# Seven block products instead of eight in the output product of a maxout layer, with the sums on VectorE

## The chip, the cores and the metric

The kernel runs on one core of a Trainium2 chip. The metric is the device time of one execution in microseconds (us). PE is TensorE, DVE is VectorE, ACT is ScalarE, POOL is GpSimd, SP is SyncE, whose queue issues most of the transfers.

## What is computed

Two layers, one after the other. The first is a DeltaNet attention, a recurrence over 768 positions with a state of 48 x 48 per head, for 4 sequences and 8 heads. The second is a maxout layer on the 3072 tokens that come out, with 384 features each:

```python
for t in range(S):
    y[:, :, t] = np.einsum('bhd,bhde->bhe', q[:, :, t], state)
    v_old = np.einsum('bhde,bhd->bhe', state, kt)
    state = state + bt[:, :, :, None] * np.einsum('bhd,bhe->bhde', kt, vt - v_old)
...
h = np.maximum(np.maximum(x @ w1, x @ w2), x @ w3)
return (h @ w_out).astype(np.float32)
```

x is 3072 x 384, w1 to w3 are 384 x 768, w_out is 768 x 384. All is FP32.

## The kernel before, in words

The positions are taken in chunks of 64, which turns the recurrence into matrix products and one triangular system of 64 x 64 per chunk and head. Six groups of two chunks follow one another. A group has 512 tokens (4 sequences, two chunks of 64 positions), so that the maxout layer of a group has four sets of 128 tokens.

The order of all instructions is written by hand: the program order is the order on every engine and on every queue. `ffn(m)` (L903) makes the maxout layer of group m and yields between its products. At each yield the loop over `ffn(m)` (L1173 to L1186) puts in pieces of other work: the recurrence of group m+1 by the table `LINKS` (L1064), and steps of the triangular solve of group m+2 by `some(solving, n)` (L1186).

`ffn(m)` for a group from the second on:
- Yields 0 to 11: for each of six sets of 128 hidden features, the products with w2 - w1 and w3 - w1 (L914, `p_h`, 3 products of 512 columns each). ScalarE takes the first with a Relu (L924), VectorE the second with a maximum (L928). The hidden values are six tiles `h` of 128 x 512. The part h takes from w1 is added afterwards: `both_layers` (L891, called in the second group) multiplies w1 by w_out once, and the result lies in `w_sb[0][:, :, 0:384]`.
- Yields 12 to 19: the output product (L938 to L956). For each of four sets of 128 tokens, `p_o` sums six products of h with w_out and three of x (`xt`) with w1 w_out, each of 384 columns (L946). ScalarE copies `p_o` to `o_sb` (L952), and SyncE stores it (L955). There is a yield within each set and one after it.

`p_h`, `p_o` and `p_m` share two PSUM buffers with the tag "ffn" (L81), which are used in turn. The work of the recurrence uses three others ("two").

VectorE's part of the solve, `solve(m)` (L498): norms, then 31 steps of a product (L552, to `tmp`, two buffers) and a subtraction (L556), of 31 to 256 columns, each of which needs the one before it. Then SyncE stores the result (L577) and reads it back transposed into `ut` (L586), for which `join_z` (L694, letter z) of the next group waits at its yield 3. The solve of group m+2 begins at yield 8 of `ffn(m)`, with one step there and three at each later yield. Groups 4 and 5 (counted from 0) have no solve beside them.

Other work at the yields that the text names: y1 (`to_y`, L793, VectorE adds `p_y` at L803), x1 (`y_blocks`, L833, stores y), w0 and w1 (`read_y`, reads it back), X0 and X1 (`turn_y`, L857, VectorE's transposes into the next group's `xt`, L861), s1 (`step`, L771, VectorE adds `p_s` to the state, L789), u1 (`new`, `p_u`, L759), k1 and q1 (L738, L747; VectorE subtracts `p_k` from `v_t`, L743), P0 (`prep_values`, GpSimd scales `v_t`, L287), K0 to K3 (loads of keys on GpSimd's queue, L120). "square" (L308) is a ring of 17 tiles of 128 x 512 for h and the recurrence's intermediates.

Of the kernel before, what the change touches and what calls it, by code (L numbers as in the profile page):

```python
# [9 lines left out]
FP32 = mybir.dt.float32  # L10
# [4 lines left out]
ALU = mybir.AluOpType  # L15

C = 64
# [6 lines left out]
def kernel(  # L24
# [47 lines left out]
    work = ctx.enter_context(tc.tile_pool(name="work", bufs=2))  # L72
# [7 lines left out]
    def ps_ffn(shape, name):  # L80
        return psum.tile(shape, FP32, name=name, tag="ffn", bufs=2)  # L81
# [27 lines left out]
    def rows(bb):  # L109
        return slice(C * bb, C * (bb + 1))  # L110
# [77 lines left out]
    t1 = [const.tile([128, 2, H, BL], FP32, name=f"t1{i}") for i in range(NU)]  # L188
# [118 lines left out]
    def square(name):  # L307
        return work.tile([128, H, C], FP32, name=name, tag="square", bufs=17)  # L308
# [189 lines left out]
    def solve(m):  # L498


        x = in_rows(xs[m])
# [38 lines left out]
        for j in range(size - 1):  # L540
            a, b = j + 1, size - 1 - j
            n = BL // size
            tmp = work.tile([128, 256], FP32, name="tmp")
            t_v = tmp[:, 0 : n * a * b].rearrange("p (s c i) -> p s c i", s=n, i=b)
            row, column, rest = (
                xv[:, :, j, None, j + 1 : size],
                yv[:, :, 0:a, j, None],
                yv[:, :, 0:a, j + 1 : size],
            )
            if n == 1:  # L550
                row, column, rest, t_v = (t[:, 0] for t in (row, column, rest, t_v))
            nc.vector.tensor_tensor(  # L552
                out=t_v, in0=row.to_broadcast(t_v.shape),
                in1=column.to_broadcast(t_v.shape), op=ALU.mult,
            )
            nc.vector.tensor_tensor(out=rest, in0=rest, in1=t_v, op=ALU.subtract)  # L556
            if m == 1 and j == BL - 8:
                nc.scalar.copy(done[:, :, 0:HB], y[:, :, 0:HB])
            elif m == 1 and j == BL - 2:
                nc.vector.tensor_copy(done[:, :, HB:BL], y[:, :, HB:BL])  # L560
            yield
        if m == 0:
# [3 lines left out]
            for i in range(4):  # L566
                if i % 2:
                    n = H * (i == 3)
# [7 lines left out]
        for cc in range(2):  # L576
            nc.sync.dma_start(  # L577
                out=y_d[cc].rearrange("f b h i j -> (f b h) i j"),
                in_=done[64 * cc : 64 * (cc + 1)],
            )  # L580
        yield
        for cc in range(2):
            for half in range(2):
                for bb in range(2):
                    r0 = C * bb + BL * half
                    (one_queue if m or cc else both_queues)[bb].dma_start(  # L586
                        out=ut[cc][
                            r0 : r0 + BL, :, :, BL * half : BL * (half + 1)
                        ].rearrange("p g h i -> p (g h) i"),
                        in_=y_d[cc, half, 2 * bb : 2 * bb + 2].rearrange(  # L590
                            "b h c i -> c (b h) i"
                        ),
# [126 lines left out]
    xts, rhss, qss, us, yts = {}, {}, {}, {}, {}  # L719
# [171 lines left out]
    def both_layers(t):  # L891
        p_m = ps_ffn([128, DM], "p_m")
        for f in range(FT):
            nc.tensor.matmul(  # L894
                p_m,
                w_sb[0][:, t, f * 128 : (f + 1) * 128],
                wo_sb[:, f],
                start=(f == 0),
                stop=(f == FT - 1),
            )  # L900
        nc.scalar.copy(w_sb[0][:, t, 0:DM], p_m)

    def ffn(m):  # L903
        xt = xts[m]
        hs = {}

        def hidden(f, lo, w):
            if f not in hs:
                hs[f] = square("h").rearrange("p h c -> p (h c)")
            h = hs[f][:, lo : lo + w]  # L910
            for i in range(m > 0, 3):
                p_h = ps_ffn([128, TOK], "p_h")[:, 0:w]
                for t in range(KT):
                    nc.tensor.matmul(  # L914
                        p_h,
                        w_sb[i][:, t, f * 128 : (f + 1) * 128],
                        xt[:, t, lo : lo + w],
                        start=(t == 0),
                        stop=(t == KT - 1),
                    )  # L920
                if i == 0:
                    nc.scalar.copy(h, p_h)
                elif m and i == 1:
                    nc.scalar.activation(  # L924
                        out=h, in_=p_h, func=mybir.ActivationFunctionType.Relu
                    )
                else:
                    nc.vector.tensor_tensor(out=h, in0=h, in1=p_h, op=ALU.max)  # L928
                yield


        early = FT // 2 if m == 0 else 0
        for lo in (0, TOK // 2):
            for f in range(early):
                yield from hidden(f, lo, TOK // 2)
        for f in range(early, FT):
            yield from hidden(f, 0, TOK)
        for i in range(4):  # L938
            cc, g = divmod(i, 2)
            p_o = ps_ffn([128, DM], "p_o")  # L940
            last = slice(i * 128, (i + 1) * 128)
            terms = [(hs[f][:, last], wo_sb[:, f]) for f in range(FT)]
            if m:
                terms += [(xt[:, t, last], w_sb[0][:, t, 0:DM]) for t in range(KT)]
            for n, (stays, moves) in enumerate(terms):
                nc.tensor.matmul(  # L946
                    p_o, stays, moves, start=(n == 0), stop=(n == len(terms) - 1)
                )
                if m and n == 4:
                    yield  # L950
            o_sb = work.tile([128, DM], FP32, name="o_sb")
            nc.scalar.copy(o_sb, p_o)  # L952
            for bb in range(2):
                tok0 = (2 * bb + g) * S + (2 * m + cc) * C
                nc.sync.dma_start(out=out[tok0 : tok0 + C, :], in_=o_sb[rows(bb)])  # L955
            yield  # L956
# [3 lines left out]
    def some(gen, n):  # L960
        for _ in range(n):
            if next(gen, gen) is gen:
                break

    conv = weights()
    solving = solve(0)
    zeros(*(t[:, :, :, D:DP] for t in kmore), qall[:, :, :, D:DP])
    for t in (*ut, st):
# [69 lines left out]
    for _ in range(2):  # L1038
# [15 lines left out]
    to_y(0)  # L1054
    halves_t(1)
    solving = solve(1)
    some(solving, 1)
    to_x(0)
# [5 lines left out]
    LINKS = {  # L1064
# [3 lines left out]
    }  # L1068
    EARLY_LINKS = {
# [19 lines left out]
        t=turn, K=load_k, L=lambda n: load_blocks(n, nc.sync),  # L1089
        g=lambda n: gram(n, queues=(nc.gpsimd,) * 2 if n in (10, 11) else one_queue),  # L1090
# [29 lines left out]
    for i, _ in enumerate(ffn(0)):  # L1120
# [17 lines left out]
        if i == 20:  # L1138
            solving = solve(2)
            some(solving, 1)  # L1140
# [32 lines left out]
    for m in range(1, GROUPS):  # L1173
        for i, _ in enumerate(ffn(m)):
            if i == 0:
                some(solving, 3)
            if m == 1 and i in (2, 5, 8):
                both_layers(i // 3)
            if m + 2 < GROUPS:
                if i == 6:  # L1180
                    blocks(m + 2)
                if i == 8:
                    solving = solve(m + 2)
            links(m + 1, LINKS.get(i, ""))
            if i > 7:
                some(solving, 3 if i > 8 else 1)  # L1186
    by_hand.close()
# [1 line left out]
_INS = ['q', 'k', 'v', 'beta', 'moe_w1', 'moe_w2', 'moe_w3', 'moe_w_out']  # L1189
# [26 lines left out]
```

## Time and profile before

| | |
|---|---|
| median of 3 runs | 518.06 us (516.55 to 520.37) |
| the profiled execution, its own time | 523.32 us |
| its span, first to last instruction | 521.3 us |
| TensorE busy | 496.0 us (95%) |
| VectorE, GpSimd, ScalarE busy | 306.0, 192.6, 163.3 us |
| L914 `p_h`, instructions, busy | 522, 220.7 us |
| L946 `p_o`, instructions, busy | 288 with h (97.7 us), 120 with x (42.0 us) |
| L552 and L556, the solve's steps | 139 and 139 instructions on `y_bl`, 51.4 and 48.5 us |
| L952, ScalarE's copies of `p_o` | 24, 11.5 us, 479 ns each |
| mean granted clock of TensorE | 0.966 |

Every matrix product of FP32 operands stands in the profile as two instructions: 204 products `p_o` in the program are 408 rows. "Busy" is the time in which an engine has an instruction in flight. In a timeline row the numbers are the start, the time from the start of the first to the end of the last instruction in it, the engine and the line; in brackets stands the idle time before it and what ended it. Durations of TensorE's rows run into one another, so that the distance from start to start is the time that a product takes.

### The profile page before, as it was taken

What the parts mean: (1) busy time and instruction counts of PE and PEld (TensorE: products, weight loads), DVE (VectorE), ACT (ScalarE), POOL (GpSimd) and SP (SyncE); (2) the same over time, 40 slices, a digit from 0 to 9 for tenths busy, and PEclk for the clock granted to TensorE, in tenths of its full rate; (3) what the DMA queues carried; (4) which work ended last, traced back from release to release, by engine and by line L of the source; (5) the groups of instructions that cost most, each with busy time, mean ns of one, the idle gap of its engine ahead of it and who ended that gap; (6) DMA issues with size and microseconds to landing.
All of it is one profiled execution on the core that took longest, in us unless ns stands there. A gap on an engine that the chain in (4) does not pass through costs nothing.

```text
span 521.3 us, 18005 instructions
## 1 busy us (share of the span) xinstructions
PE 496.0 (95%) x7836; PEld 306.0 (59%) x7836; DVE 306.0 (59%) x689; ACT 163.3 (31%) x302; POOL 192.6 (37%) x317
## 2 busy tenths in 40 slices
PE   7578799998999999999999999999999999999996
PEld 6467688755565555665555565555655555654453
DVE  5888969867996430998642987635896321111100
ACT  4575755883422242201243101252101411011000
POOL 6435462783391926670665680503130000000000
PEclk9956989999999999999989999999999999999999
DMA  8927969764055925353675354823343202220011
GB/s 116 205 37 208 209 136 149 189 192 106 2 132 141 180 49 130 102 129 84 148 126 123 107 144 95 169 38 92 83 106 83 41 3 63 62 60 0 0 30 30
DMA packets 105277, 53.45 MB, mean 103 GB/s; under 512 B 89712, under 2 KB 98960, under 8 KB 105200
## 3 DMA queue, kind: packets, MB, share of 16 engines
q1 hardware_dynamic: 93616, 31.55, 30.0%
q0 software_dynamic: 9472, 20.37, 15.9%
q8 instruction: 61, 1.00, 0.8%
q10 hardware_dynamic: 2112, 0.39, 0.5%
q14 instruction: 16, 0.13, 0.1%
HBM read 39.17 MB, written 13.11 MB: 100 GB/s over the span
## 4 chain that ended last, share of the span: by engine, by line
PE 80%; DMA 7%; DVE 6%; ACT 2%; issue 2%; SPq 2%; POOL 1%; DVEq 0%; ACTq 0%; POOLq 0%
PE p_h L914 35%; PE p_o L946 26%; PE p_g L406 2%; PE p_u L759 2%; PE p_m L894 2%; PE p_k L731 2%; PE p_q L731 2%; PE p_y L801 2%; DMA kmore<-in_k_dram 2%; PE p_s L782 2%; PE p_j L714 2%; DMA x_bl<-at_d 2%; DMA qall<-in_q_dram 1%; DMA ut<-y_d 1%; SPq L120 1%
## 5 line engine op out<-in xcount | busy, mean ns | idle before, releaser
L914 PE MATMUL p_h<-xt,w_sb 128*128 128x512 f32 (+1 forms) x522 | 220.7, 567 | 1.9 <-issue 1.2
L914 PEld LDWEIGHTS p_h<-xt,w_sb 128*128 128x128 f32 x522 | 96.6, 194 | 88.2 <-issue 81.1
L946 PE MATMUL p_o<-wo_sb,h 128*128 128x384 f32 x288 | 97.7, 489 | 0.0
L928 DVE TENSOR_TENSOR h<-h,p_h 128x512 f32<-128x512 f32 (+1 forms) x48 | 29.6, 617 | 93.6 <-PE p_h L914 93.0
L946 PEld LDWEIGHTS p_o<-wo_sb,h 128*128 128x128 f32 x288 | 53.7, 190 | 35.7 <-issue 0.5
L552 DVE TENSOR_TENSOR tmp<-x_bl,y_bl 128x31 f32<-128x31 f32 (+20 forms) x139 | 51.4, 370 | 4.1
L952 ACT COPY o_sb<-p_o 128x384 f32<-128x384 f32 x24 | 11.5, 479 | 132.1 <-PE p_o L946 126.0
L556 DVE TENSOR_TENSOR y_bl<-y_bl,tmp 128x31 f32<-128x31 f32 (+20 forms) x139 | 48.5, 349 | 4.8
L924 ACT ACTIVATE h<-p_h 128x512 f32<-128x512 f32 x30 | 17.9, 597 | 90.3 <-PE p_h L914 87.3
L946 PE MATMUL p_o<-w_sb,xt 128*128 128x384 f32 x120 | 42.0, 486 | 0.0
L364 POOL DMA_DIRECT2D turned<-in_q_dram x72 | 39.3, 554 | 5.4 <-POOL turned L359 3.1
L254 POOL TENSOR_TENSOR w_sb<-mant,up 128x384 int32<-128x384 int32 x18 | 18.8, 1046 | 41.1 <-DVE mant L250 39.0
L946 PEld LDWEIGHTS p_o<-w_sb,xt 128*128 128x128 f32 x120 | 22.8, 190 | 15.9
L406 PEld LDWEIGHTS p_g<-kqt 48*64 48x64 f32 x1216 | 24.3, 141 | 9.9 <-issue 6.4
L406 PE MATMUL p_g<-kqt 48*64 48x64 f32 (+1 forms) x1216 | 27.5, 240 | 0.9 <-ACT kqt L335 0.8
L120 POOL DMA_DIRECT2D kpad<-in_k_dram x32 | 21.9, 692 | 13.8 <-issue 12.7
L789 DVE TENSOR_TENSOR st<-st,p_s 48x768 f32<-48x768 f32 (+1 forms) x18 | 17.1, 950 | 15.3 <-PE p_s L782 15.1
L139 POOL DMA_DIRECT2D v_t<-in_v_dram x14 | 11.6, 832 | 38.1 <-PE p_u L759 38.1
L390 DVE TENSOR_TENSOR pt<-p_g,mask 128x512 f32<-128x512 f32 x20 | 13.8, 689 | 16.1 <-PE p_g L406 15.8
L287 POOL TENSOR_TENSOR v_t<-v_t,nrm 128x768 f32<-128x768 f32 x12 | 17.9, 1495 | 9.0 <-DVE nrm L281 8.9
L359 POOL MEMSET turned<- 128x96 f32 x18 | 3.3, 192 | 46.6 <-DVE kqt L380 46.6
L759 PEld LDWEIGHTS p_u<-v_t,ut 64*64 64x64 f32 x768 | 14.2, 149 | 8.9 <-issue 6.4
(143 smaller groups left out, 616.4 us busy)
## 6 DMA issues: line engine op xcount, KB each, us to landing
out_dram<-o_sb SPq DMA_DIRECT2D x48, 96.0 KB, 2.2
w_bits<-in_moe_w_dram SPq DMA_DIRECT2D x9, 384.0 KB, 6.0
w_bits<-in_moe_w_dram POOLq DMA_DIRECT2D x9, 384.0 KB, 5.6
turned<-in_q_dram POOLq DMA_DIRECT2D x72, 48.0 KB, 2.8
kpad<-in_k_dram POOLq DMA_DIRECT2D x32, 96.0 KB, 5.9
y_x<-y SPq DMA_DIRECT2D x16, 192.0 KB
qall<-y_x SPq DMA_DIRECT2D x32, 96.0 KB, 2.6
v_t<-in_v_dram POOLq DMA_DIRECT2D x14, 192.0 KB, 4.8
```

The lines of the kernel that those rows point to most:

```text
L120: queues[bb].dma_start(out=dst[rows(bb ^ g), :, 0:D], in_=src[2 * bb + g, :, c * C : (c + 1) * C, :].rearrange("h p d -> p h d"),)
L254: nc.gpsimd.tensor_tensor(out=dst.bitcast(I32), in0=mant_v.bitcast(I32), in1=up_v, op=ALU.add)
L287: nc.gpsimd.tensor_tensor(out=vts[c], in0=vts[c], in1=nrm[:, :, :, None].to_broadcast([128, 2, H, D]), op=ALU.mult,)
L364: (queue, nc.gpsimd)[i].dma_start(out=t[p0 : p0 + 32, bb, at : at + NP * 2 * D].rearrange("p (j x) -> p j x", j=NP), in_=(k, q)[i][2 * bb ...
L406: nc.tensor.matmul(p_g[rows(bb ^ (g * i)), par, c0 : c0 + C * (1 + whole)], kq[:, 0], kq if whole else kq[:, i],)
L552: nc.vector.tensor_tensor(out=t_v, in0=row.to_broadcast(t_v.shape), in1=column.to_broadcast(t_v.shape), op=ALU.mult,)
L556: nc.vector.tensor_tensor(out=rest, in0=rest, in1=t_v, op=ALU.subtract)
L731: nc.tensor.matmul(p_b[rows(bb), par, c0 : c0 + D], kqt[g][dims(par), j, bb ^ g, i], st[dims(par), bb ^ g, g, j],)
L759: nc.tensor.matmul(p_v[rows(bb ^ g), g, i], ut[c % NU][rows(bb), g, h], rhs[rows(bb), g, h],)
L914: nc.tensor.matmul(p_h, w_sb[i][:, t, f * 128 : (f + 1) * 128], xt[:, t, lo : lo + w], start=(t == 0), stop=(t == KT - 1),)
L928: nc.vector.tensor_tensor(out=h, in0=h, in1=p_h, op=ALU.max)
L946: nc.tensor.matmul(p_o, stays, moves, start=(n == 0), stop=(n == len(terms) - 1))
```

## The change

From the second group on, `ffn` leaves the output product to a new function, `outputs`. It takes h as 2 x 2 blocks (256 tokens of one chunk by 384 hidden features: a11, a12, a21, a22, each three tiles of 128 x 256) and w_out as 2 x 2 blocks (384 hidden features by 192 columns), and makes the product of the two by Winograd's form of Strassen's scheme: seven block products instead of eight. Each block product is six products of 192 columns: two sets of 128 tokens, three tiles of hidden features. The four products of x with w1 w_out, also of 192 columns, are summed in PSUM with a12 b21, with s124 b22 and with a22 t4; the fourth stands alone.

The sums of blocks of h and of the results are made by VectorE: twelve of 128 x 256 (six s, then three and three that change s in place) and eight of 128 x 384 per group. Four PSUM tiles per group are copied by ScalarE, and four are taken by VectorE within a sum. The sums of blocks of w_out are made once, by `cross_weights` at yields 9 and 10 of the second group, partly into the columns of `w_sb[0]` that are no longer used. Each of the four output blocks (256 tokens by 192 columns) is stored by two transfers on SyncE's queue.

`outputs` has eleven yields instead of eight, so that the table `LINKS` and the number of solve steps per yield are changed: three steps up to yield 12, then two, and three at the last. `tmp` has one buffer instead of two.

```diff
-            tmp = work.tile([128, 256], FP32, name="tmp")
+            tmp = work.tile([128, 256], FP32, name="tmp", bufs=1)
...
+    def cross_weights(part):
+        left, right = slice(0, HALF), slice(HALF, DM)
+        top, bottom = wo_sb[:, 0:PAIRS], wo_sb[:, PAIRS:FT]
+        spare = w_sb[0][:, :, DM : 2 * DM]
+        minus = nc.vector.tensor_tensor
+        if part == 0:
+            minus(
+                out=spare[:, :, right], in0=bottom[:, :, right], in1=top[:, :, right],
+                op=ALU.subtract,
+            )
+            minus(
+                out=top[:, :, right], in0=top[:, :, right], in1=top[:, :, left],
+                op=ALU.subtract,
+            )
+            return
+        minus(
+            out=spare[:, :, left], in0=bottom[:, :, right], in1=top[:, :, right],
+            op=ALU.subtract,
+        )
...
+        for j in range(PAIRS):
+            minus(
+                out=fourth[j], in0=wo_sb[:, PAIRS + j, left], in1=spare[:, j, left],
+                op=ALU.subtract,
+            )
...
+    def outputs(m, hs):
+        xt, w = xts[m], crossed
+        a11, a21, a12, a22 = (
+            [hs[j + d][:, lo : lo + 256] for j in range(PAIRS)]
+            for d, lo in ((0, 0), (0, 256), (PAIRS, 0), (PAIRS, 256))
+        )
+        p, q = (ps_ffn([128, 2, HALF], "p_o") for _ in range(2))
+        def times(to, a, b, start=True, stop=True):
+            for g in range(2):
+                for j in range(PAIRS):
+                    nc.tensor.matmul(
+                        to[:, g], a[j][:, 128 * g : 128 * (g + 1)], b[j],
+                        start=(start and g == j == 0),
+                        stop=(stop and g == 1 and j == PAIRS - 1),
+                    )
...
+        times(p, a11, w["b11"])
+        m1 = held("m1", 1)
+        nc.scalar.copy(m1, p)
+        yield
+        sums = [square("s").rearrange("p h c -> p (h c)") for _ in range(PAIRS)]
+        s124, s3 = ([s[:, lo : lo + 256] for s in sums] for lo in (0, 256))
+        for j in range(PAIRS):
+            op(s3[j], a11[j], a21[j], minus)
+        for j in range(PAIRS):
+            op(s124[j], a21[j], a22[j], plus)
+        times(q, a12, w["b21"], True, False)
+        yield
+        x_times(q, 0, 0)
+        c11 = held("o_sb", 2)
+        op(c11, m1, q, plus)
+        store(c11, 0, 0)
+        yield
+        times(p, s3, w["t3"])
+        m7 = held("o_sb", 2)
+        nc.scalar.copy(m7, p)
+        yield
+        times(q, s124, w["t1"])
+        m5 = held("up", 2)
+        nc.scalar.copy(m5, q)
+        for j in range(PAIRS):
+            op(s124[j], s124[j], a11[j], minus)
+        yield
+        x_times(p, 0, 1, True, False)
+        yield
+        times(q, s124, w["t2"])
+        m6 = held("up", 2)
+        nc.scalar.copy(m6, q)
+        for j in range(PAIRS):
+            op(s124[j], a12[j], s124[j], minus)
+        yield
+        times(q, a22, w["t4"], True, False)
+        op(m6, m6, m1, plus)
+        op(m7, m7, m6, plus)
+        op(m6, m6, m5, plus)
+        op(m5, m5, m7, plus)
+        yield
+        x_times(q, 256, 0)
+        op(m7, m7, q, plus)
+        store(m7, 1, 0)
+        yield
+        times(p, s124, w["b22"], False)
+        op(m6, m6, p, plus)
+        store(m6, 0, 1)
+        yield
+        x_times(q, 256, 1, True)
+        op(m5, m5, q, plus)
+        store(m5, 1, 1)
+        yield
...
+        if m:
+            yield from outputs(m, hs)
+            return
...
-        11: "u1 w0", 13: "y1 x1 s1", 14: "X0 w1", 16: "P0", 17: "X1 K0 K1 K2 K3",
+        11: "u1 w0", 12: "y1", 13: "x1 s1", 15: "X0 w1", 18: "P0", 20: "X1 K0 K1 K2 K3",
...
+            if m == 1 and i in (9, 10):
+                cross_weights(i - 9)
...
-                some(solving, 3 if i > 8 else 1)
+                some(solving, 1 if i == 8 else 3 if i < 13 or i == 22 else 2)
```

`x_times` is the same as `times` with three tiles of x and of w1 w_out. `op` is VectorE's tensor_tensor.

More of the change, by code (lines that the diff above doesn't have):

```diff
@@ L901, in both_layers @@
         nc.scalar.copy(w_sb[0][:, t, 0:DM], p_m)
+    HALF = DM // 2
+    PAIRS = FT // 2
+    crossed = {}
+    def cross_weights(part):
[17 more added lines that the diff above has]
+        )
+        fourth = []
+        for n in range(2):
+            t = work.tile([128, DM], FP32, name="mant", bufs=2)
+            for i in range(2 - n):
+                fourth.append(t[:, HALF * i : HALF * (i + 1)])
+        for j in range(PAIRS):
[3 more added lines that the diff above has]
+            )
+        crossed.update(
+            b11=[top[:, j, left] for j in range(PAIRS)],
+            b21=[bottom[:, j, left] for j in range(PAIRS)],
+            b22=[bottom[:, j, right] for j in range(PAIRS)],
+            t1=[top[:, j, right] for j in range(PAIRS)],
+            t2=[spare[:, j, left] for j in range(PAIRS)],
+            t3=[spare[:, j, right] for j in range(PAIRS)],
+            t4=fourth,
+        )
@@ new lines, in outputs, with x_times, held, store @@
+    def outputs(m, hs):
[12 more added lines that the diff above has]
+                        stop=(stop and g == 1 and j == PAIRS - 1),
+                    )
+        def x_times(to, lo, right, start=False, stop=True):
+            times(
+                to,
+                [xt[:, t, lo : lo + 256] for t in range(KT)],
+                [w_sb[0][:, t, HALF * right : HALF * (right + 1)] for t in range(KT)],
+                start, stop,
+            )
+        def held(name, dtype_bufs):
+            return work.tile([128, 2, HALF], FP32, name=name, bufs=dtype_bufs)
+        def store(o, cc, right):
+            cols = slice(HALF * right, HALF * (right + 1))
+            s0 = (2 * m + cc) * C
+            for bb in range(2):
+                nc.sync.dma_start(
+                    out=out.rearrange("(b s) d -> b s d", s=S)[
+                        2 * bb : 2 * bb + 2, s0 : s0 + C, cols
+                    ].rearrange("g c x -> c g x"),
+                    in_=o[rows(bb)],
+                )
+        def op(to, a, b, how):
+            nc.vector.tensor_tensor(out=to, in0=a, in1=b, op=how)
+        plus, minus = ALU.add, ALU.subtract
+        times(p, a11, w["b11"])
[51 more added lines that the diff above has]
+        yield
@@ L941, in ffn @@
             last = slice(i * 128, (i + 1) * 128)
[L942 to L945, printed above, removed]
+            for f in range(FT):
                 nc.tensor.matmul(
-                    p_o, stays, moves, start=(n == 0), stop=(n == len(terms) - 1)
+                    p_o, hs[f][:, last], wo_sb[:, f], start=(f == 0), stop=(f == FT - 1)
                 )
-                if m and n == 4:
-                    yield
             o_sb = work.tile([128, DM], FP32, name="o_sb")
```

## The prediction, made before the changed kernel was run

> **What bounds the kernel now.** I read the page first (busy shares, chain), then the matrix products by line, then the busy time of each engine in the stretch of every group's output product, then the instructions one by one around the ends of those stretches.
>
> ```profile
> span 521.3 us, 18005 instructions
> ...
> PE 496.0 (95%) x7836; PEld 306.0 (59%) x7836; DVE 306.0 (59%) x689; ACT 163.3 (31%) x302; POOL 192.6 (37%) x317
> ...
> PE p_h L914 35%; PE p_o L946 26%; PE p_g L406 2%; PE p_u L759 2%; PE p_m L894 2%; PE p_k L731 2%; PE p_q L731 2%; PE p_y L801 2%; DMA kmore<-in_k_dram 2%; PE p_s L782 2%; PE p_j L714 2%; DMA x_bl<-at_d 2%; DMA qall<-in_q_dram 1%; DMA ut<-y_d 1%; SPq L120 1%
> ```
>
> TensorE bounds it: the output product (L946) alone is 26% of the chain. VectorE looks half idle, but that is an average. The busy table of the output stretches of groups 1 to 5 (columns: stretch, length, then PE, PEld, DVE, ACT, POOL):
>
> ```profile
> 221.00:246.30 25.30, 25.30 (x206) 15.44 (x201) 23.33 (x47) 2.24 (x4) 9.87 (x16) 1.00 0.46 116
> 296.80:322.20 25.40, 25.40 (x209) 15.49 (x202) 21.97 (x50) 2.24 (x4) 14.18 (x24) 1.00 0.53 129
> 369.60:394.90 25.30, 25.30 (x208) 15.26 (x201) 22.51 (x44) 2.24 (x4) 4.20 (x5) 1.00 0.33 84
> 438.20:462.80 24.60, 24.60 (x141) 14.73 (x138) 3.33 (x3) 2.24 (x4) 0.00 (x0) 1.00 0.27 67
> 493.70:521.30 27.60, 23.35 (x73) 13.46 (x71) 0.69 (x1) 1.92 (x4) 0.00 (x0) 0.98 0.13 29
> ```
>
> In groups 1, 2 and 3 VectorE, which solves the triangular systems there (L552, L556), is busy 22 to 23.3 us of 25.3, almost as long as TensorE. Only in groups 4 and 5 is it free. The timelines at the end of group 2's stretch, VectorE's, TensorE's and SyncE's queue:
>
> ```profile
> 304.11 0.95 DVE L803 TENSOR_TENSOR y<-qs,p_y 128x768 f32<-128x768 f32 x1 [1.98 <-PE p_y L801]
> ...
> 323.67 0.21 DVE L556 TENSOR_TENSOR y_bl<-y_bl,tmp 128x31 f32<-128x31 f32 x1
> ```
> ```profile
> 296.83 4.14 PE L946 MATMUL p_o<-wo_sb,h 128*128 128x384 f32 x12
> ...
> 322.17 2.74 PE L914 MATMUL p_h<-xt,w_sb 128*128 128x512 f32 x6
> ...
> 336.99 1.35 PE L701 MATMUL p_z<-ut,at 32*32 32x32 f32 x128
> ```
> ```profile
> 324.12 1.19 SPq L577 DMA_DIRECT2D y_d<-y_bl  x2
> 327.26 4.74 SPq L586 DMA_DIRECT2D ut<-y_d  x8
> ```
>
> The solve ends at 323.88, 1.7 us after TensorE has begun the next group. Its result goes out at 324.1, comes back to ut by 331.5 + 0.5 + 3.9 (landing) = 335.9, and TensorE wants it at 337: about 1 us of slack. For group 1 the same chain is 1.2 us late already; for group 3 it is just in time. So VectorE's work in these stretches is not covered: what is added shows within 1 to 3 us.
>
> **What the Trainium skill says.** "TensorE: Matmul & The Clock Gate", Back-to-back issue gap: N/2.4 + 2.5 ns. Here an FP32 product is recorded as two instructions, and the trace fits 2N/2.4 + 2.5 for each: 430 ns at N=512 (2.58 us for six), 322.5 at 384 (3.87 for twelve), 217 at 256. "VectorE: DVE Perf Modes", TRN2 errata: an FP32 tensor_tensor takes (N+151)/0.96 ns; the trace agrees, 0.42 us at 255 and 0.69 at 512. "SBUF — State Buffer", Terms: VectorE and GpSimd share a port pair, locked for a whole instruction, "the loser fully blocks". The trace agrees: the step of 0.37 us at 222.91 took 2.62 us across GpSimd's 1.49 us product (L287, at 223.81), one at 380.62 took 2.80 across 381.65.
>
> **Part 1: the products.** Before, a group has 4 x 9 products of 384 columns, 72 instructions: 23.23 us in the last group. After: seven block products of 6 plus four x-products of 6, 66 products of 192 columns, 132 instructions. No row shows 192 columns. Lower bound by columns: 2 x 192/2.4 + 2.5 = 162.5 ns, together 21.5 us, a gain of 1.75. Upper bound by the weight load's recorded 190 ns: 25.1 us, a loss of 1.9. I take the lower: six transposes, each with a load of its own (recorded 202 ns), pass in 0.66 us, 110 ns apiece, so loads overlap. Gain 1.75 per group.
>
> **Part 2: VectorE's sums.** Per group twelve sums of 256 columns and eight of 384. Where the next instruction doesn't need the result, the pitch in the trace is about 0.09 us below the duration (0.59 for 512, 0.47 for 384 at L871), which gives 0.34 for 256. So 12 x 0.34 = 4.1, 8 x 0.47 = 3.8: 7.9 us. Bounds: 6.4 (columns at 0.96 GHz alone) and 10.1 (0.46 and 0.57, waits between all). ScalarE still makes four copies of 384 columns, as before: nothing.
>
> **Part 3: crossing the weights,** once, in group 1 at yields 9 and 10: three subtractions of 576 columns (0.67 us, between 512's and 768's 0.87) and three of 192 (0.27 plus waits): 2.9 us. They stand before v_t's subtraction (218.05), for which p_u (219.92) waits. VectorE has worked without a gap there since 209.02, so all 2.9 count.
>
> **Part 4: new waits on TensorE.** The two PSUM buffers p and q are now read by VectorE in program order, between solve steps. I follow group 2, on the clock of before. TensorE: first product 296.83 to 298.8, p_y to 299.9, q with a12 to 301.8, p_s to 302.5, q with x to 304.5. VectorE: y at 300.0, three steps to 303.4, six sums to 305.5, state (1.94) to 307.4, two steps to 309.2, c11 to 309.75. Only then is q free: the third block product (to m7) ended at 306.5, so TensorE waits 3.3. The next to 311.8, x into p to 313.8. VectorE: two steps to 311.5, transpose X0 1.17, two steps to 314.5, three differences to 315.6: TensorE waits 1.9. Product to 317.65; q's next product waits for ScalarE's copy (0.48 + 0.25): 0.7. Then x to 322.3, b22 to 324.25. VectorE: two steps, two steps, three differences to 320.15, two steps, four sums to 323.9, two steps to 325.3, m7 to 325.75: TensorE waits 1.6 for q. VectorE: X1, two steps, m6 to 328.7: the next group's first p_h, which takes p's buffer, begins at 328.8 instead of 322.17. VectorE ends at 330.8 instead of 323.88. Behind m6 stand two steps, m5 and the last step, 2 us. So VectorE runs through without a gap, and its sum sets both ends.
>
> **The sum.** With that lag of 2.0 us between the next p_h and the end of the solve:
> - Group 1: end 248.82 + 7.9 + 2.9 - 0.65 (idle before X1, gone) = 259.0; next p_h 257.0 instead of 246.3, +10.7. Two stores of m5 now stand on SyncE's queue right ahead of the solve's result (about 0.7 us), while the lag shrinks from 2.5 to 2.0: +0.2 on the late chain. +10.9.
> - Group 2: 323.88 + 7.9 - 1.5 (most of the 1.98 idle before y) = 330.3, next p_h +6.2 (6.6 step by step). GpSimd's product at 304.2 met only y from PSUM; now it meets sums from SBUF. 2.3 us if so, which I take at a bit over half: +1.3. +7.6.
> - Group 3: 398.96 + 7.9 - 1.5 = 405.4, next p_h 403.4 instead of 394.95: +8.4, more than in group 2 because there the solve ended 4.0 after TensorE's start.
> - Groups 4 and 5: no solve. All sums fit beside the products of 1.95 us; only the wait for ScalarE's copy of m6 (0.7) shows. 0.7 - 1.75 = -1.0 each. At the very end VectorE's last sum and a store stand for ScalarE's copy and a store: nothing.
>
> 10.9 + 7.6 + 8.4 - 2.0 = 24.9. The profiled span of 521.3 becomes 546; the execution's 523.32, 548. Its own time is 5 above the median of 518.06, but what I add is mostly VectorE's, whose durations don't depend on that: median 543.
>
> Costed at nothing: one tmp buffer instead of two (every step already waits for the one before it; gap 0.04 us); stores of half rows, same bytes, covered by some 10 us before their buffers return; three more "square" tiles per group (17 in 17 buffers, each reused by its own successor a group later; if one were late, TensorE or ScalarE would wait for it up to a microsecond); later y1, X0, X1, P0 and K (X1 is done at 327, before p_h). If K or P0 came too late, p_s or v_t of the next group would wait, but these have 15 us.
>
> **Rivals.**
> - Less: VectorE's sums cost their columns only and GpSimd's product meets none of them: 4.5 less over three groups, 1.3 less, and the 2.4 us blocks in groups 1 and 3 fall in waits, up to 4.8 less. 533 to 537. For it: shorter pitches of independent operations. Chance 0.2.
> - More: the weight load sets 190 ns (3.6 us more in each of groups 4 and 5; hidden behind VectorE in the others), or sums with waits at 10.1 (6.6 more), or the clock of TensorE falls in gaps of over 3 us: "TensorE: Matmul & The Clock Gate", HAM oscillation, has the rule "no PE-idle gaps >~3.4µs", and the trace of before has no such gap in these stretches. 548 to 555. Chance 0.17.
> - Faster: the sums are hidden. Then 5 x 1.75 less 5 x 0.7 remains: -5, 513. It needs VectorE to have room: the stretch after would last 23.6 us, VectorE has 22 to 23.3 of its own, and the chain behind the solve 1 us. It decides if the sums cost less than about 2 us a group, 0.1 us apiece; a 256-column operation takes four times that. Chance 0.03, with 0.02 for within 1%.
> - My forecast, 537 to 548: 0.58.
>
> Range: without the last and the far end of the others, 534 to 551. One per cent, about what a measurement here can tell from no change, is 5.2 us; so faster 0.03, same 0.02, slower 0.95.
>
> **What would show it.** Right: output stretches of groups 1 to 3 at 30 to 36 us with VectorE busy over 90% and TensorE waiting for VectorE's c11, differences, m7 and m6; stretches 4 and 5 about 1 us shorter than before; 192-column products at 163 ns; 256-column sums at 0.42 us. Wrong: TensorE without gaps in groups 1 to 3, products at 190 ns, or p_z waiting for ut many microseconds more than before.

## The result, and the profile after

The changed kernel takes 542.14 us (median of 4 runs, 540.26 to 546.25), the kernel before 519.03 on the same chip (4 runs, 516.55 to 520.37): the ratio is 1.0462 with an interval of 1.0387 to 1.0537. Ratios here compare the fast runs of the two kernels and aren't quite the quotients of the medians. Forecast were 543 us, and slower. The profiled execution took 542.75 us.

The page of the kernel after, span, busy time of each engine, and the chain of work that ended last, by engine and by line:

```profile
span 540.8 us, 18737 instructions
...
PE 498.8 (92%) x8136; PEld 352.5 (65%) x8136; DVE 349.0 (65%) x795; ACT 163.4 (30%) x302; POOL 192.7 (36%) x317
...
PE 57%; DVE 26%; DMA 6%; ACT 4%; issue 3%; SPq 2%; POOL 0%; DVEq 0%; ACTq 0%; POOLq 0%
PE p_h L1057 31%; PE p_o L960 7%; DVE tmp L552 6%; DVE y_bl L556 5%; DMA qall<-in_q_dram 4%; PE p_g L406 3%; PE p_o L1089 3%; DVE s L989 2%; PE p_m L894 2%; DVE st L789 2%; PE p_u L759 2%; SPq L120 2%; PE p_k L731 1%; PE p_j L714 1%; DVE xt L861 1%
```

The chain shows what the busy shares hide. TensorE is still at 92%, VectorE at 65%, but VectorE's share of the chain went from 6% to 26%, and the solve's steps (L552, L556) and the sums (L989), which weren't among its lines, now are. The output product fell from 26% to 10% (L960 and L1089).

The busy table of the output stretches of groups 1 to 5 in the kernel after, with the columns of the table of before:

```profile
222.05:255.27 33.22, 26.63 (x267) 24.56 (x260) 31.78 (x72) 2.71 (x5) 7.66 (x12) 0.95 0.29 72
302.90:336.40 33.50, 26.78 (x267) 24.77 (x261) 31.55 (x71) 2.71 (x5) 14.05 (x24) 0.95 0.38 92
383.99:416.36 32.37, 27.47 (x267) 25.95 (x261) 30.62 (x71) 2.71 (x5) 4.19 (x5) 0.89 0.25 58
459.29:482.95 23.66, 23.09 (x202) 22.52 (x197) 11.42 (x22) 2.71 (x5) 0.00 (x0) 1.00 0.26 64
513.86:540.80 26.94, 21.88 (x133) 21.28 (x131) 9.33 (x21) 1.91 (x4) 0.00 (x0) 0.99 0.13 30
```

The first three grew from about 25.3 to 33.2, 33.5 and 32.4 us, and VectorE works 94 to 96% of each; TensorE has gaps now. The last two became 0.94 and 0.95 us shorter (the fifth measured to TensorE's last instruction: 22.44 after, 23.39 before).

TensorE's timeline in group 2's stretch, kernel after (start, length, what; in brackets the idle time before it and what ended it):

```profile
309.14 2.22 PE L960 MATMUL p_o<-w_sb,xt 128*128 128x192 f32 x12
312.45 2.19 PE L960 MATMUL p_o<-w_sb,s 128*128 128x192 f32 x12 [1.10 <-DVE s L989]
318.26 3.87 PE L960 MATMUL p_o<-wo_sb,s 128*128 128x192 f32 x12 [3.62 <-DVE o_sb L989]
321.93 2.19 PE L960 MATMUL p_o<-w_sb,xt 128*128 128x192 f32 x12
...
326.63 2.22 PE L960 MATMUL p_o<-mant,h 128*128 128x192 f32 x12 [0.57 <-ACT up L1023]
...
333.67 2.22 PE L960 MATMUL p_o<-w_sb,xt 128*128 128x192 f32 x12 [0.92 <-DVE o_sb L989]
336.40 2.84 PE L1057 MATMUL p_h<-xt,w_sb 128*128 128x512 f32 x6 [0.51 <-DVE up L989]
```

Every wait but one ends on a sum of VectorE: the s that the next block product multiplies, c11 (`o_sb`) before the buffer q is free again, m7, and m6 (`up`) before the next group may begin. VectorE's timeline over the same stretch:

```profile
306.32 0.95 DVE L803 TENSOR_TENSOR y<-qs,p_y 128x768 f32<-128x768 f32 x1 [0.56 <-PE p_y L801]
...
309.33 2.65 DVE L556 TENSOR_TENSOR y_bl<-y_bl,tmp 128x240 f32<-128x240 f32 x1
311.90 2.09 DVE L989 TENSOR_TENSOR s<-h 128x256 f32<-128x256 f32 x6
...
317.65 0.55 DVE L989 TENSOR_TENSOR o_sb<-m,p_o 128x384 f32<-128x384 f32 x1
...
337.92 0.21 DVE L556 TENSOR_TENSOR y_bl<-y_bl,tmp 128x31 f32<-128x31 f32 x1
```

Six sums take 2.1 us, and between y and the end of the solve no bracket stands. The step at 309.33 should take 0.41 us: it met GpSimd's product of 1.49 us (L287, at 310.21). c11 is done at 318.20. TensorE had ended its last product for c11 at 311.4 and the next one, into p, at 314.6; it then waits 3.6 us.

### The profile page after: what moved, and what is told of

It reads as the page before. It is cut to its first block, busy times and chain, and to the rows that moved or that the text cites. A ratio compares the mean times of both kernels' runs of the same rounds, so it can differ in the third digit from the quotient of the medians.

```text
span 540.8 us, 18737 instructions
## 1 busy us (share of the span) xinstructions
PE 498.8 (92%) x8136; PEld 352.5 (65%) x8136; DVE 349.0 (65%) x795; ACT 163.4 (30%) x302; POOL 192.7 (36%) x317
## 4 chain that ended last, share of the span: by engine, by line
PE 57%; DVE 26%; DMA 6%; ACT 4%; issue 3%; SPq 2%; POOL 0%; DVEq 0%; ACTq 0%; POOLq 0%
PE p_h L1057 31%; PE p_o L960 7%; DVE tmp L552 6%; DVE y_bl L556 5%; DMA qall<-in_q_dram 4%; PE p_g L406 3%; PE p_o L1089 3%; DVE s L989 2%; PE p_m L894 2%; DVE st L789 2%; PE p_u L759 2%; SPq L120 2%; PE p_k L731 1%; PE p_j L714 1%; DVE xt L861 1%
## 5 line engine op out<-in xcount | busy, mean ns | idle before, releaser
L556 DVE TENSOR_TENSOR y_bl<-y_bl,tmp 128x31 f32<-128x31 f32 (+20 forms) x139 | 50.7, 365 | 4.8
L552 DVE TENSOR_TENSOR tmp<-x_bl,y_bl 128x31 f32<-128x31 f32 (+20 forms) x139 | 49.6, 357 | 3.4
L960 PE MATMUL p_o<-w_sb,xt 128*128 128x192 f32 x240 | 43.8, 334 | 2.0 <-DVE o_sb L989 2.0
L960 PEld LDWEIGHTS p_o<-w_sb,xt 128*128 128x128 f32 x240 | 40.5, 195 | 2.8 <-DVE o_sb L989 2.6
L960 PE MATMUL p_o<-wo_sb,s 128*128 128x192 f32 x120 | 26.6, 382 | 11.0 <-DVE o_sb L989 11.0
L960 PEld LDWEIGHTS p_o<-wo_sb,s 128*128 128x128 f32 x120 | 24.3, 227 | 11.9 <-DVE o_sb L989 11.9
L960 PE MATMUL p_o<-w_sb,s 128*128 128x192 f32 x120 | 21.3, 328 | 1.9 <-DVE s L989 1.9
L960 PE MATMUL p_o<-wo_sb,h 128*128 128x192 f32 x120 | 21.8, 333 | 0.0
L960 PEld LDWEIGHTS p_o<-w_sb,s 128*128 128x128 f32 x120 | 19.7, 190 | 2.4 <-issue 2.4
```

Source lines behind the costliest of these rows:

```text
L552: nc.vector.tensor_tensor(out=t_v, in0=row.to_broadcast(t_v.shape), in1=column.to_broadcast(t_v.shape), op=ALU.mult,)
L960: nc.tensor.matmul(to[:, g], a[j][:, 128 * g : 128 * (g + 1)], b[j], start=(start and g == j == 0), stop=(stop and g == 1 and j == PAIRS - 1),
```

## The experiments

The theory: in groups 1 to 3 VectorE sets both ends of the stretch, so that each microsecond of sums is a microsecond of time, whoever waits for it. Rival A: the sums themselves cost little, and the tie of two PSUM buffers to VectorE's order makes the waits. Rival B: the long waits halve TensorE's clock, and this is what is paid. Rival C: the solve between the sums delays the sums, and its work could stand elsewhere. "Before" is in each case the kernel before, measured beside it on the same chip: 518.32 us for the first four experiments, 518.0 for the next two, 517.2 for the last three. Of the diffs only the core is shown.

### The twelve sums of h left out

```diff
-        for j in range(PAIRS):
-            op(s3[j], a11[j], a21[j], minus)
-        for j in range(PAIRS):
-            op(s124[j], a21[j], a22[j], plus)
+        s124, s3 = a22, a21
...
-        for j in range(PAIRS):
-            op(s124[j], s124[j], a11[j], minus)
...
-        for j in range(PAIRS):
-            op(s124[j], a12[j], s124[j], minus)
```

> The changed kernel without the twelve sums of 256 columns per group (the products take blocks of h as they are, so the result is not that of the layer); the eight sums of 384 columns, the PSUM hand-over and the order of the rest stay. Theory (VectorE's amount of work beside the solve sets the pace): 12 x 0.34 = 4.1 us less in each of groups 1 to 3, nothing in groups 4 and 5: 542 - 12 = 530 (527 to 533), output stretches of groups 1 to 3 from 33 to about 29 us. Rival A (TensorE's waits for its two PSUM buffers, p and q, set it, not the amount): these waits stay, only the ones for s of about 1 us go: 538 to 541. Rival B (the clock of TensorE after the waits): as A.

Measured: 533.25 us, ratio 1.0304 (1.0252 to 1.0355), just above the theory's 527 to 533. The stretches are 29.52, 27.79 and 29.74 us, together 12.0 less than after, where three times the 4.1 us of these sums make 12.3. By group it is 3.7, 5.7 and 2.6, since GpSimd's product (L287) now falls elsewhere: in group 2 it lengthens a step by 0.24 us instead of 2.24, in group 3 by 2.20 instead of 1.08. Without this, 3.7 to 3.8 us remain in each group, 11.2 in all: a little less than the sums took. Waits for c11 remain, 2.6, 1.0 and 2.9 us, but shorter. Rival A, under which the time should have stayed near that of after, falls. The time fell by less than 12, because one later stretch grew: between group 2's first `p_h` and its first `p_o` (below, such a stretch is called hidden, since it makes the hidden values) 52.0 us pass instead of 47.6. What is late there, on ScalarE and on TensorE:

```profile
292.74 0.26 ACT L261 ACTIVATE root_bl<-x_bl 128x32 f32<-128x32 f32 x1 [4.00 <-DMA x_bl<-at_d]
```
```profile
298.03 4.53 PE L1048 MATMUL p_h<-xt,w_sb 128*128 128x512 f32 x6 [1.70 <-DVE h L1062]
```

TensorE reaches group 2 earlier, but the next solve's input `x_bl` doesn't. ScalarE stands 4.0 us before it, and what is queued behind that instruction, the Relu of h, comes late to VectorE and TensorE; six `p_h` then take 4.46 us from start to start instead of 2.77, at a low clock.

### The first six sums made twice

```diff
-        for j in range(PAIRS):
-            op(s3[j], a11[j], a21[j], minus)
-        for j in range(PAIRS):
-            op(s124[j], a21[j], a22[j], plus)
+        for j in range(2 * PAIRS):
+            op(s3[j % PAIRS], a11[j % PAIRS], a21[j % PAIRS], minus)
+        for j in range(2 * PAIRS):
+            op(s124[j % PAIRS], a21[j % PAIRS], a22[j % PAIRS], plus)
```

> The changed kernel with the first six sums of 256 columns made twice in each group, to the same place with the same values. Theory (amount of VectorE's work): 6 x 0.34 = 2.0 us more in each of groups 1 to 3, nothing in 4 and 5, where VectorE is idle: 542 + 6 = 548 (546 to 550). Rival A (the hand-over of the PSUM buffers): the first sums are ahead of only one hand-over, and other waits would shrink: 542 to 544.

Measured: 545.25 us, ratio 1.0558 (1.0491 to 1.0625): 3 us more than after by the medians, 5 by the ratios, just below the theory's 546 to 550 and above the rival's 542 to 544. The intervals of the two ratios overlap, so the stretches decide. They are 35.27, 35.35 and 33.28: 2.05, 1.85 and 0.9 more, where the six take 2.02; groups 4 and 5 stay at 23.67 and 22.45. In group 3:

```profile
391.63 4.11 DVE L989 TENSOR_TENSOR s<-h 128x256 f32<-128x256 f32 x12
```

GpSimd's product (L287, at 395.32) now meets the end of these sums and the state's sums, which read PSUM; no step is held, where after one took 1.50 us instead of 0.42. In group 2 the held step takes 2.45 instead of 2.65. With these differences taken out, the three groups grew by 2.0 us each. So with VectorE full the six cost their own length, and nothing where VectorE is free.

### The solve's steps moved behind the stretch

```diff
-                some(solving, 1 if i == 8 else 3 if i < 13 or i == 22 else 2)
+                some(solving, 1 if i == 8 else 3 if i < 13 else 21 if i == 22 else 0)
```

> The changed kernel with no solve steps between the products from yield 13 on; all that remain come after the last product of the group. The amount of VectorE's work is the same. Theory (amount): the output stretches of groups 1 to 3 shrink to 24 or 25 us, but the solve ends later (in group 2 about 15 us after the stretch) and its result is on the way for another 12 us, so that the next group waits for the maximum and for ut: total the same or up to 8 us longer, 541 to 552. Rival A (the interleaving of solve steps with the PSUM hand-over costs the time, not the amount): 9 us less in each of three groups: 515 to 528.

Measured: 565.66 us, ratio 1.0932 (1.0886 to 1.0978), 24 us more than after. The time of the rival (C here, rival A in the expectation) is missed by far, and the theory's range too, by 14 us. The stretches shrank, to 28.09, 28.21 and 25.92, but the three hidden stretches behind them grew, from 47.6, 47.6 and 42.9 to 59.97, 60.76 and 57.38. VectorE's timeline, group 1:

```profile
240.23 1.10 DVE L989 TENSOR_TENSOR s<-h,s 128x256 f32<-128x256 f32 x3 [2.80 <-PE p_o L960]
...
245.67 0.56 DVE L989 TENSOR_TENSOR o_sb<-o_sb,p_o 128x384 f32<-128x384 f32 x1 [1.89 <-PE p_o L960]
...
264.85 0.95 DVE L743 TENSOR_TENSOR v_t<-v_t,p_k 128x768 f32<-128x768 f32 x1
```

Without steps to fill them, VectorE has waits of its own for TensorE, 6.9 us in this stretch (0.52, 2.80, 1.89, 0.25 and 1.40). My expectation had counted VectorE's work as if it ran through. The solve ends at 264.9 instead of 257.0, the subtraction from `v_t` stands behind it, and so does what is needed for `p_g`, which waits and then runs slowly, 4.14 us instead of 2.02:

```profile
266.87 4.21 PE L406 MATMUL p_g<-kqt 48*64 48x128 f32 x96 [7.41 <-DVE kqt L380]
```

So rival C gains nothing in this form: here the two engines' waits for each other are no longer filled with the solve, and moving it behind costs more than it brings. Places between the two weren't tried. The run also shows that VectorE's amount of work, which is the same here, doesn't set the time alone: it does so only where VectorE runs without a gap.

### The crossing of the weights earlier

```diff
-            if m == 1 and i in (2, 5, 8):
-                both_layers(i // 3)
-            if m == 1 and i in (9, 10):
-                cross_weights(i - 9)
+            if m == 1 and i in (1, 3, 5):
+                both_layers(i // 2)
+            if m == 1 and i in (6, 7):
+                cross_weights(i - 6)
```

> The changed kernel with the product of w1 and w_out at yields 1, 3 and 5 of the second group instead of 2, 5 and 8, and the sums of the weights' blocks at yields 6 and 7 instead of 9 and 10, in a stretch where VectorE waits for TensorE for 6 us. Theory: the 2.9 us (2.26 + 0.76 us of waits of TensorE) leave the unbroken run of VectorE: 542 - 3 = 539 (538 to 540.5). Rival: these 2.9 us were hidden: 542.

Measured: 541.0 us, ratio 1.0457 (1.041 to 1.0505), not to be told from after by ratio. The 2.26 us of the expectation is 2.16 in the trace after. In this run's trace the move did work where it was made: `p_u` doesn't wait, and from group 1's first `p_h` to group 2's 92.1 us pass instead of 94.3, 2.2 less. The next hidden stretch gives 1.25 of it back, again at the next solve's input: ScalarE waits for it 3.27 us, 2.10 in the kernel after, and TensorE then waits for the maximum behind it:

```profile
296.09 2.84 PE L1057 MATMUL p_h<-xt,w_sb 128*128 128x512 f32 x6 [0.90 <-DVE h L1071]
```

About 1 us remains, less than these runs can show. What one stretch saves isn't what the kernel saves, while a chain beside it keeps its own time.

### Seven products only in groups 4 and 5

```diff
-        if m:
+        if m >= 4:
             yield from outputs(m, hs)
...
-            if m == 1 and i in (9, 10):
-                cross_weights(i - 9)
+            if m == SEVEN and i in (3, 4):
+                cross_weights(i - 3)
```

Here SEVEN is 4. Groups 1 to 3 have the old output product, the old `LINKS` and the old three steps per yield.

> Seven block products only in groups 4 and 5, which have no solve beside them; groups 1 to 3 as before the change, with the order of before; the sums of the weights' blocks at yields 3 and 4 of group 4, where VectorE is idle. Theory: the products' own gain less the wait for ScalarE's copy of m6, as the two stretches show it in the changed kernel: 0.94 + 0.70 = 1.6 us less than before: 517.4 beside 519.0 (ratio 0.995 to 0.999). Rival (192-column products cost more than they save anywhere, the weight loads): 519 to 522.

Measured over 22 runs: 516.5 us, ratio 0.9978 (0.9955 to 1.0001), as forecast, though the interval just reaches no change. The stretches are 25.34, 25.34, 25.32, then 23.72 and 22.45: −0.88 and −0.94. One wait is left in each, for ScalarE's copy of m6, which frees the buffer q. From the timeline of group 5:

```profile
497.20 2.11 PE L960 MATMUL p_o<-w_sb,s 128*128 128x192 f32 x12
499.89 2.22 PE L960 MATMUL p_o<-mant,h 128*128 128x192 f32 x12 [0.57 <-ACT up L1023]
```

### The same with a third PSUM buffer

```diff
-        times(q, a22, w["t4"], True, False)
+        q4 = ps_two("p_o4")[:, 0, 0:DM].rearrange("p (g x) -> p g x", g=2)
+        times(q4, a22, w["t4"], True, False)
...
-        x_times(q, 256, 0)
-        op(m7, m7, q, plus)
+        x_times(q4, 256, 0)
+        op(m7, m7, q4, plus)
```

The block product with t4 goes to a tile of the recurrence's ring ("two"), which has little to do by then.

> As the run before it, and the product with t4 with the x-product that follows goes to a third PSUM tile (of the recurrence's three), so that it doesn't wait for ScalarE's copy of m6. Theory: the wait of 0.57 us in each of the two groups goes: another 1.1 us less, 516.3 beside 519.0 (ratio 0.993 to 0.997). Rival (the wait only moves to the next hand-over): as the run before it.

Measured over 10 runs: 514.69 us, ratio 0.9928 (0.9897 to 0.996). The stretches of groups 4 and 5 are 22.83 and 21.61 us, −1.77 and −1.78: the 1.75 us that the products alone were to bring. Group 5 again:

```profile
501.71 2.11 PE L960 MATMUL p_o<-mant,h 128*128 128x192 f32 x12
503.66 2.11 PE L960 MATMUL p_o<-w_sb,xt 128*128 128x192 f32 x12
```

No bracket, and 1.95 us from product to product. This version is faster than both kernels, by 0.4 to 1.0% than the kernel before.

### The changed kernel again, as measure for the next two

> The changed kernel once more, to stand beside the two runs sent with it on the same chip: ratio to before 1.040 to 1.053, output stretches of groups 1 to 3 of 32 to 34 us, with the granted clock at 0.5 to 0.7 in the product that follows the wait for c11.

Measured: 542.08 us, ratio 1.0481 (1.0449 to 1.0513), stretches 33.32, 33.33, 32.38, 23.66 and 22.45. The granted clock in the product after the wait for c11 was 0.74, 0.50 and 0.63 in groups 1 to 3, the first of them above the expected range.

### The same steps, spread so that no wait is long

```diff
-                some(solving, 1 if i == 8 else 3 if i < 13 or i == 22 else 2)
+                some(solving, {8: 1, 12: 2, 13: 1, 14: 3, 15: 1, 16: 3, 17: 3, 22: 3}.get(i, 3 if i < 12 else 2))
```

> The changed kernel with other numbers of solve steps at yields 12 to 17 (2, 1, 3, 1, 3, 3 instead of 3, 2, 2, 2, 2, 2), so that c11 comes about 1.8 us earlier and TensorE waits for it about 1.8 us instead of 3.6; the same work in all. Theory (amount of VectorE's work sets the pace, and TensorE's slow clock after the long wait is hidden behind it): no change, within 1.5 us of the changed kernel. Rival B (the clock that falls after the wait costs time: 1.6, 1.7 and 2.9 us in the three groups): 4 to 6 us less than the changed kernel.

Measured: 543.84 us, ratio 1.0516 (1.046 to 1.0572), not to be told from the changed kernel. The waits for c11 became shorter, but not as short as the 1.8 us expected: 2.69, 3.21 and 2.89. Group 1, TensorE:

```profile
232.20 2.22 PE L960 MATMUL p_o<-wo_sb,s 128*128 128x192 f32 x12 [2.69 <-DVE o_sb L989]
234.25 2.11 PE L960 MATMUL p_o<-w_sb,xt 128*128 128x192 f32 x12
...
249.45 2.22 PE L960 MATMUL p_o<-w_sb,xt 128*128 128x192 f32 x12 [3.38 <-DVE o_sb L989]
252.18 2.84 PE L1057 MATMUL p_h<-xt,w_sb 128*128 128x512 f32 x6 [0.52 <-DVE up L989]
```

Behind the wait of 2.69 us, and behind that of 3.38, the clock held: the product after the first took 2.05 us from start to start instead of 3.5. Yet the stretch is 33.30 us long as before: TensorE waits 3.38 us for m7 instead. In a group where the low clock is avoided nothing is gained, so rival B falls for group 1. For the other two, the two profiles of the changed kernel can be laid side by side. Group 3, the repeat:

```profile
396.91 3.46 PE L960 MATMUL p_o<-wo_sb,s 128*128 128x192 f32 x12 [3.82 <-DVE o_sb L989]
400.16 2.60 PE L960 MATMUL p_o<-w_sb,xt 128*128 128x192 f32 x12
```

Here the slow products lost 1.8 us against 1.95 each, 2.9 in the first profile, and the stretches are 32.38 and 32.37 us long. In group 2 it is the other way round, 2.9 and 1.8, and 33.33 and 33.50. So what the clock takes there is hidden too.

Spreading didn't keep the clock everywhere: in group 2 a wait of 3.21 us and in group 3 waits of 2.89 and 2.75 lowered it. The last of these is before the stretch's final product, which nothing hides. It took 3.73 us, where product and wait for m6 together take 2.7 in group 1: 1.0 us of the 1.9 by which this stretch grew (34.26). The other 0.9 is a solve step that GpSimd's product held to 2.39 us instead of 1.50.

### The sums of h on GpSimd

```diff
-        def op(to, a, b, how):
-            nc.vector.tensor_tensor(out=to, in0=a, in1=b, op=how)
+        def op(to, a, b, how, engine=nc.vector):
+            engine.tensor_tensor(out=to, in0=a, in1=b, op=how)
...
-            op(s3[j], a11[j], a21[j], minus)
+            op(s3[j], a11[j], a21[j], minus, nc.gpsimd)
```

The other nine sums of 256 columns likewise.

> The changed kernel with the twelve sums of 256 columns on GpSimd instead of VectorE. If the two engines work independently, VectorE has 4.1 us less in each of groups 1 to 3: 9 to 12 us less than the changed kernel, as in the run without these sums, provided the sums come in time. If GpSimd's product locks VectorE's path to the memory, as the step of 2.26 us beside L287 suggests, each sum there (0.5 to 0.6 us, from 1.49 us for 768 columns) stops VectorE for at least as long as VectorE's own would have taken: 12 x 0.55 = 6.6 us instead of 4.1, less where VectorE waits or reads PSUM: the changed kernel's time or up to 10 us more. I expect the second, and more on top in groups 4 and 5 where the slower sums hold up the products.

Measured: 548.93 us, ratio 1.0609 (1.0563 to 1.0656), 6.9 us more than the changed kernel beside it. The stretches are 34.54, 35.40, 36.38, and for groups 4 and 5 unchanged 23.66 and 22.45. GpSimd's timeline, then VectorE's, group 1:

```profile
223.91 3.93 POOL L989 TENSOR_TENSOR s<-h 128x256 f32<-128x256 f32 x5 [2.01 <-PE p_y L801]
```
```profile
223.73 0.36 DVE L556 TENSOR_TENSOR y_bl<-y_bl,tmp 128x192 f32<-128x192 f32 x1
224.13 0.78 DVE L552 TENSOR_TENSOR tmp<-x_bl,y_bl 128x207 f32<-128x207 f32 x1
225.65 0.94 DVE L803 TENSOR_TENSOR y<-qs,p_y 128x768 f32<-128x768 f32 x1
```

GpSimd takes 0.73 us for a sum of 256 columns, up to 1.04 beside VectorE's work, and VectorE's steps beside it take twice their 0.36 to 0.4 us; y, which reads PSUM, isn't stretched. Over the whole kernel VectorE's busy time fell only from 349.0 to 345.5 us, though sixty sums, about 20 us of it, had left it. The 6.9 us aren't the price of this alone: in groups 1 and 3 the stretch's final product ran at half clock, 4.0 us instead of 2.2, behind waits of 4.03 and 5.10 us for m7. The extra time expected in groups 4 and 5 didn't appear.

## Why the prediction was right, and where its terms were off

**What bounds.** VectorE bounds groups 1 to 3, as forecast: busy 94 to 96%, TensorE waiting for the sums named. Sums left out or made twice move the stretches by about their own length, once the difference that GpSimd's product makes is taken out (3.7 to 3.8 for 4.0 in each group; 2.0 for 2.02).

**The products.** 162.5 ns per instruction was right: twelve in 1.95 us. The upper bound by the weight load's 190 ns falls. With the third buffer the whole 1.75 us per group appeared.

**The sums.** 7.9 us per group forecast; in group 1 the twelve of 256 took 4.0 (six in 2.02, twice three in 1.0), the eight of 384 together 4.1 (c11 0.47, four dependent ones 2.24, three 0.46 each): 8.1.

**Crossing the weights.** Forecast 2.9 us, all of it counting; measured 3.06 in all (1.46 and 1.60), with 2.16 of wait at `p_u`. Not all of it counted: group 1's hidden stretch grew by 2.2.

**The waits on TensorE** (forecast for group 2; measured in groups 1, 2, 3): s 0.1 (0.76, 1.10, 0), c11 3.3 (3.61, 3.62, 3.81), copy of m6 0.7 (0.62, 0.57, 0.57), m7 1.6 (1.09, 0.92, 0), next `p_h` 1.0 (0.52, 0.51, 0.53). The wait of 1.9 for the three differences didn't appear: the product ahead of it ran at half clock and filled the time. The waits that did appear come to 6.6, 6.7 and 4.9 us, and with the 1.6, 1.8 and 2.9 us that the slow products lost to 8.2, 8.5 and 7.8, where the forecast for group 2 adds up to 8.6. Which waits appear was less certain than this sum, which VectorE sets.

**The groups.** From first `p_h` to first `p_h`, group 1 grew by 10.1 us (84.2 to 94.3; forecast 10.7, without the 0.2 below). In group 2 the stretch grew by 8.2 where 7.6 was forecast (6.2 + 1.3 makes 7.5, the count step by step 7.9): the mis-sized term is GpSimd's block, taken at a bit over half of 2.3 (1.3), which came in full, 2.65 us for a step of 0.41 (in the repeat 2.46, for a sum). In group 3 it grew by 7.05, where 8.4 was forecast. The same term, the other way: before, a step was held to 2.80 us there, and I left that as it was; after, the step that meets GpSimd's product takes 1.50. The difference, 1.3, is what is missing. Groups 4 and 5: −0.94 and −0.95 for −1.0.

**The late chain.** Of group 1's result I had said +0.2 us for the next group. The two profiles show −2.9 (group 2's hidden stretch 50.51 before, 47.63 after). That isn't the change's doing, since both kernels with the old code in groups 1 to 3 take 47.40 and 47.36 there. The profiled execution of before, 4 to 5 us above the kernel's median, had this on TensorE:

```profile
263.33 0.72 PE L701 MATMUL p_z<-ut,at 32*32 32x32 f32 x60 [1.18 <-DMA ut<-y_d]
263.98 4.54 PE L914 MATMUL p_h<-xt,w_sb 128*128 128x512 f32 x6
```

Six `p_h` in 4.5 us instead of 2.77, behind a wait for ut. What I read as a chain already late was in good part an event of one execution.

**The sum.** The spans differ by 19.5: −1.2 (TensorE comes to group 1 earlier), +10.1, −2.9, +8.2, +0.1, +7.05, −0.3, −0.94, −0.95, and +0.2 at the end. Without the −2.9 it is 22.4; the medians differ by 23.1, and 24.9 was forecast. Of the 1.8 us too many, group 3's term gives 1.35 and group 1's 0.8 (0.6 because the crossing counted less, and the 0.2 for the late chain), and group 2's takes 0.6 off; the rest is within what single executions differ by. That 543 lies within 1 us of the measured 542.1 is in part luck: the 24.9 was 1.8 too much, and the median it was added to, 518.06, was 1 us below the 519.03 measured beside the changed kernel.

**The rivals on record.** "Faster" failed where the prediction put the point: the sums cost 8 us a group, not 2. "Less" failed on both its terms: the sums cost more than their columns, and GpSimd's product still met a step in each of the three groups (2.26, 2.65 and 1.50 us). Of "more", the clock did fall, which I had put at 548 to 555, but the low clock is hidden behind VectorE.

**Open.** Why some waits left the clock alone and others of the same length didn't wasn't tried further. Nor was it tried to bring `x_bl` forward, which took back part of two experiments.

## What to carry to other kernels

Before giving work to an engine that looks half idle, read its busy time in the very stretch where the work will land: VectorE at 59% of the span was at 86 to 92% there, and 8 us of sums bought 1.75 us of products. The same exchange pays where the other engine is truly free and no buffer waits on it: in the two groups without a solve, with a third PSUM buffer, it makes the kernel 0.7% faster (0.4 to 1.0%). And a gain in one stretch counts only up to the next chain beside it, such as the input of the next solve here.

## What the hardware showed that was not expected

TensorE's granted clock after the wait for c11, kernel after, group 1 and then group 3 (stretch, length, busy time of PE, PEld, DVE, ACT, POOL, then the granted clock):

```profile
237.10:240.60 3.50, 3.47 (x12) 3.47 (x13) 3.36 (x7) 0.00 (x0) 0.00 (x0) 0.57 0.37 84
240.60:242.60 2.00, 2.00 (x14) 2.00 (x13) 1.93 (x7) 0.48 (x1) 0.00 (x0) 1.00 0.69 147
...
398.20:402.20 4.00, 3.99 (x12) 4.00 (x13) 3.83 (x8) 0.00 (x0) 0.00 (x0) 0.50 0.41 90
402.20:405.00 2.80, 2.80 (x13) 2.80 (x13) 2.66 (x8) 0.48 (x1) 0.00 (x0) 0.68 0.38 89
```

A wait of 3.6 to 3.8 us is followed by 3.5 to 4 us at about half clock, in group 3 by 2.8 more at 0.68. The Trainium skill, "TensorE: Matmul & The Clock Gate", HAM oscillation, puts the limit of a harmless gap at about 3.4 us. Here gaps of 3.21, 2.89 and 2.75 us (steps spread) and of 2.60 us (sums left out) lowered the clock too, while 2.69 and 3.38 did not. A gap of 3.38 us in group 1 of the repeat did (0.74, then 0.66), and behind the waits of 1.18 and 1.70 us shown above, before group 2's slow six `p_h` in the kernel before and with the sums left out, the clock was 0.62. So the length of the single gap doesn't decide, and one below 3.4 us isn't safe. The lock between VectorE and GpSimd ("SBUF — State Buffer", Terms) is confirmed step by step in the last experiment, and its price depends on when the step begins. GpSimd's same product of 1.49 us held steps of 0.3 to 0.4 us to between 0.62 and 2.80; in all traces but that of the last experiment, a step or sum held by it ended 0.17 to 0.29 us after it. In the kernel after, the steps that began 2.1, 2.4 and 1.2 us before that end took 2.26, 2.65 and 1.50 us.
